# Retention and squared-ReLU FFN on one core: other idle matmuls, a merged first product, and work moved between the steps of the first block

## The chip, the cores and the metric

The kernel runs on one core of a Trainium2 chip. The metric is the device time of one execution in microseconds. A core has a matrix engine (PE, with its weight loads shown apart as PEld), a vector engine (DVE), a scalar engine (ACT), a general engine (POOL), a queue for transfers (SP), and 16 DMA engines which the queues of SP and POOL share. Each engine works through its own instructions in order and waits on semaphores for the others.

## The reference, cut to what matters

Four sequences of 768 tokens, 8 heads of 64. Each head keeps a decaying 64 x 64 state; its output goes through an FFN of width 2048 with a squared ReLU.

```python
gamma = 1.0 - 2.0 ** (-5.0 - np.arange(H))
for t in range(S):
    state = gamma[None, :, None, None] * state + np.einsum('bhd,bhe->bhde', k[:, :, t], v[:, :, t])
    y[:, :, t] = (1 / np.sqrt(D)) * np.einsum('bhd,bhde->bhe', q[:, :, t], state)
x = y.transpose(0, 2, 1, 3).reshape(B * S, H * D)        # 3072 x 512
h = np.maximum(x @ w_in, 0.0)                            # 3072 x 2048
out = (h * h) @ w_out                                    # 3072 x 512
```

## The kernel before

The 3072 tokens are 24 chunks of 128. Within a chunk the recurrence is turned into matmuls: q is scaled by powers of gamma and k by inverse powers, scores of k against q are masked to the causal half (DVE writes `pt`), the state of all earlier tokens stands in `c_ps` and is copied to `s_bd`, and the outputs are `s_bd` against q plus v against `pt`. The outputs, copied to `xt` by ACT or DVE, are the input of the FFN. Chunks are grouped into blocks for the FFN: the first has four chunks, the others two (`BLOCKS`).

There is no scheduler: the order in which the Python code issues instructions is the order on each engine (`manual_schedule`). Three parts matter here.

*The start, written out by hand from L1203.* Chunks 0 to 3 are handled as two pairs (0, 1) and (2, 3), in which a row of a tile holds two neighbouring tokens r=0 and r=1. `scale_q4`, `transpose_q4`, `scale_pair_k`, `transpose_pair_k`, `scores_pair`, `state_pair`, `outputs_pair` and `finish_pair` are the steps; `cast_pair_v(m, r)` turns the v of one r to bf16 on POOL, or on ACT with `on_scalar`. `outputs_pair` takes for each of two groups of heads first all matmuls of r=0 (eight), then those of r=1. Between the steps `keep_awake(n)` issues idle matmuls, 4n of 128 columns each, from a zeroed corner of the tile `spare` into a PSUM tile that nobody reads; `spare` is needed later for the masked scores of the second pair and for sums of the first block. `cast_w` turns quarters of w_in, which come by DMA as f32 into `stage`, to bf16, in halves of 256 columns, on the engines named by letters (V for DVE, S for ACT, G for POOL).

*The first product.* `first_product` multiplies one 128-column block f of w_in with `xt`, in four matmuls over the 512 inputs. `first_unit(tb, g, c, parts)` does the four blocks of quarter g for one chunk c, in two parts of two blocks, and then a ReLU by ACT (`relu`, L855) from PSUM into `h`; squares are taken by DVE (L826) at the next place. At the start, quarter 0 is done chunk by chunk: part 0 of chunks 0 and 1 ahead of the outputs of the second pair, part 1 after them, then chunks 2 and 3 whole. The other three quarters, f = 4 to 15, are done with 512 columns, all four chunks at once.

*The numbered places.* The FFN is a sequence of pieces, and after piece n the steps that `put` has noted for place n are issued. Places 5 to 16 follow the blocks f = 4 to 15 of the first block; 17 to 32 follow the pieces of its second product (`last_of_first`, `second_products`). There chunks 0 and 1 are done plainly, two rows f at a time (`plain`, L1039), and chunks 2 and 3 by a scheme of seven products on sums of h (`first_sums`, `third_sums`, `fourth_sums`) and of w_out (`sum_w_out`, L341), in 256-column matmuls (L1004). Its pieces are, by place: 17 to 20 plain(0) to plain(3), 21 the lower halves of two sum products, 22 and 23 plain(4) and plain(5), 24 a third lower half, 25 plain(6), 26 plain(7) followed by ACT's copy `a` of one product and two output copies, 27 two upper halves and DVE's u = product + a, 28 and 29 the product with `a12`, 30 and 31 a product that goes into the tile that u was read from, 32 the last. `third_sums` and `fourth_sums` are put at 26 and 27.

Among these pieces stand the steps of chunks 4 to 7: `attend(m, scaled, places)` puts `scale_kv` at the first place (DVE scales k, POOL casts v), `transpose_k` at the second (PE, then two ACT copies into `k_bd`, L426), the scores of two groups of heads at the third and fourth, `state` at the fourth, and `outputs` at the last (PE, then ACT's copy to `xt`, L529). From chunk 8 on another form is used (`attend2`), with half-chunk tables `kf2` and `cmask2` which `pack_constants` makes in two steps: memsets, iotas and masks on POOL, then a cast and a product on DVE and an exponential on ACT. On POOL's queue `load_w_out` issues the four quarters of w_out at places 6, 8, 11 and 14.

Of the kernel before, what the change touches and what calls it, by code (L numbers as in the profile page):

```python
# [9 lines left out]
FP32 = mybir.dt.float32  # L10
BF16 = mybir.dt.bfloat16
# [20 lines left out]
def kernel(  # L32
# [9 lines left out]
    nc = tc.nc  # L42
    P = nc.NUM_PARTITIONS
# [3 lines left out]
    C = 128  # L47
# [25 lines left out]
    hpool = ctx.enter_context(tc.tile_pool(name="hpool", bufs=3))  # L73
# [6 lines left out]
    ps_y = ctx.enter_context(tc.tile_pool(name="ps_y", bufs=1, space=bass.MemoryType.PSUM))  # L80
    ps_c = ctx.enter_context(tc.tile_pool(name="ps_c", bufs=1, space=bass.MemoryType.PSUM))
    ps_f = ctx.enter_context(tc.tile_pool(name="ps_f", bufs=4, space=bass.MemoryType.PSUM))
# [113 lines left out]
        load_w_in(g)  # L196


    spare = hpool.tile([P, 4096], BF16, name="h2")
    still = spare[:, 4096 - P : 4096]  # L200
    nc.vector.memset(still, 0.0)

    lng = const.tile([P, H], FP32)
    for h in range(H):
        nc.gpsimd.memset(lng[:, h : h + 1], float(np.log(gammas[h])))
# [34 lines left out]
    ident = const.tile([P, P], BF16)  # L240
# [115 lines left out]

    idle_ps = []

    def keep_awake(n, pool=ps_f, name="psf"):
        if not idle_ps:  # L360
            idle_ps.append(pool.tile([P, P], FP32, name=name))
        for _ in range(4 * n):
            nc.tensor.matmul(idle_ps[0][:], lhsT=still, rhs=still, start=True, stop=True)  # L363

    def end_awake():
        idle_ps.clear()
# [170 lines left out]
    def pair_view(t):  # L537
        return t.rearrange("s c hh d -> s (c hh d)").rearrange("s (r h d) -> s r h d", r=2, h=H)
# [42 lines left out]
    def cast_pair_v(m, r, on_scalar=False):  # L581
        at[m]["v"] = pair_view(v_bd2s[m // 2])
        if on_scalar:
            nc.scalar.activation(at[m]["v"][:, r], raw_v[m][:, r], AF.Copy)
        else:
            nc.gpsimd.tensor_copy(at[m]["v"][:, r], raw_v[m][:, r])
# [242 lines left out]
    h2s = {}  # L829

    def h_tiles(tb):
        wide = BLOCKS[tb] * C
        count = NFB * wide // 4096
        for _ in range(count):
            t = hpool.tile([P, 4096], BF16, name="h2")
            h2s.setdefault(tb, []).append(t.rearrange("e (f t) -> e f t", t=wide))

    def h_of(tb, f0, f1=None):
        n = NFB // len(h2s[tb])
        j, f = divmod(f0, n)  # L840
        return h2s[tb][j][:, f : f + (1 if f1 is None else f1 - f0)]

    def first_product(tb, hp, f, cols):
        g, fq = divmod(f, FPQ)
        for cb in range(NCB):
            nc.tensor.matmul(  # L846
                hp,
                lhsT=w_in_bf[g][:, cb, fq * 128 : (fq + 1) * 128],
                rhs=xts[tb][:, cb, cols],
                start=(cb == 0),  # L850
                stop=(cb == NCB - 1),
            )

    def relu(hv, hp, on_scalar=False):
        nc.scalar.activation(hv, hp[:], AF.Relu)  # L855
        squares.append((hv, on_scalar))
# [246 lines left out]
    def first_unit(tb, g, c, parts=(0, 1)):  # L1103

        if tb not in h2s:
            h_tiles(tb)
        if (tb, g, c) not in open_ps:
            open_ps[tb, g, c] = ps_f.tile([P, FPQ, C], FP32, name="psf")
        hp = open_ps[tb, g, c]
        cols = slice(c * C, (c + 1) * C)  # L1110
        half = FPQ // 2
        for part in parts:
            for fq in range(part * half, (part + 1) * half):
                first_product(tb, hp[:, fq, :], g * FPQ + fq, cols)
        if 1 in parts:
            relu(h_of(tb, g * FPQ, (g + 1) * FPQ)[:, :, cols], open_ps.pop((tb, g, c)))

    def ffn_pieces(tb):
        nch = BLOCKS[tb]
        TB = nch * C  # L1120
        if tb == 0:
            first_sums, last_sums, second_products = last_of_first()
            put(11, first_sums, 0)
            put(17, first_sums, 1)
            put(26, last_sums[0])
            put(27, last_sums[1])
            for f in range(FPQ, NFB):
                hp = ps_f.tile([P, TB], FP32, name="psf")
                first_product(tb, hp[:], f, slice(0, TB))
                relu(h_of(tb, f)[:, 0], hp)  # L1130
                yield
            yield from second_products()
            return
        elif tb <= 2:

            for c in range(nch):
                for g in range(NQ):
                    first_unit(tb, g, c)
                    if c * NQ + g in (1, 2, 3) and kept:
                        next(kept[0])  # L1140
                    if c * NQ + g == 4:
                        kept.clear()
                    if tb in SEVEN and (c, g) == (1, 3):
                        first_sums, rest = seven_products(tb)
                        first_sums(slice(0, 4))
                    yield
            if tb in SEVEN:
                yield from rest()
                return
        else:  # L1150
            h_tiles(tb)
            per = 512 // TB
            if tb in SEVEN:
                first_sums, rest = seven_products(tb)
            for f0 in range(0, NFB, per):
                hp = ps_f.tile([P, per, TB], FP32, name="psf")
                for f in range(f0, f0 + per):
                    first_product(tb, hp[:, f - f0, :], f, slice(0, TB))
                relu(h_of(tb, f0, f0 + per), hp, tb in SEVEN and f0 // per in (1, 3))
                if f0 // per in (1, 2, 3) and kept:  # L1160
                    next(kept[0])
                if f0 // per == 4:
                    kept.clear()
                if f0 // per == 5 and tb in SEVEN:
                    first_sums(slice(0, 4))
                yield
            if tb in SEVEN:
                yield from rest()
                return


        def second(op, j, g, cols=slice(0, DM)):
            for fq in range(FPQ):
                f = g * FPQ + fq
                nc.tensor.matmul(  # L1175
                    op[:],
                    lhsT=h_of(tb, f)[:, 0, j * C : (j + 1) * C],
                    rhs=w_out_bf[g][:, fq, cols],
                    start=(f == 0),
                    stop=(f == NFB - 1),  # L1180
                )

        def store(op, j, cols=slice(0, DM)):
            osb = opool.tile([P, DM], FP32, name="osb")
            nc.scalar.activation(osb[:, cols], op[:], AF.Copy)
            r0 = (first[tb] + j) * C
            nc.sync.dma_start(out[r0 : r0 + C, cols], osb[:, cols])


        for j in range(nch):  # L1190
            op = ps_f.tile([P, DM], FP32, name="psf")
            for g in range(NQ):
                second(op, j, g)
                if g == NQ - 1:
                    store(op, j)
                yield
# [3 lines left out]
    def small_pt():  # L1200
        return ptpool.tile([P, NPAIR, 2, C], BF16, name="pt").rearrange("s p hh t -> s (p hh t)")

    keep_awake(10, pool=ps_y, name="y")  # L1203
    scale_q4(0, 0)
    scale_q4(0, 1)
    transpose_q4(0, 0, *tp)
# [39 lines left out]
    state_pair(0, 1, "SV")  # L1246
    cast_w("in", 0, (0,), "GGGG")
    cast_pair_v(2, 0)
    cast_pair_v(2, 1, on_scalar=True)
    first_unit(0, 0, 0, (0,))  # L1250
    first_unit(0, 0, 1, (0,))
    cast_w("in", 0, (1,), "GGVV")
    outputs_pair(2, 0, ((ps_y, "y"), st))
    outputs_pair(2, 1)
    finish_pair(2, 0)
    state_pair(2, 0, "VV")
    first_unit(0, 0, 0, (1,))
    first_unit(0, 0, 1, (1,))
    finish_pair(2, 1, on_scalar=False)
    cast_w("in", 1, (0,), "VVGG")  # L1260
    first_unit(0, 0, 2)
# [9 lines left out]
    start = [sum(npieces[:tb]) for tb in range(len(BLOCKS) + 1)]  # L1271
    parts = {}

    def put(place, what, *args):
        parts.setdefault(place, []).append((what, args))
# [4 lines left out]
    def attend(m, scaled, places):  # L1280
        if m % 2 == 0:
            put(scaled, scale_q, m, 0)
            put(scaled + 2 if m == 4 else scaled, scale_q, m, 1)
            put(places[0], transpose_q, m)
        put(16 if m == 4 else places[0], scale_kv, m)
        put(places[1], transpose_k, m)
        put(places[2], scores, m, 0)
        put(places[3], scores, m, 1)
        put(places[3], state, m)
        put(places[4], outputs, m)  # L1290
# [23 lines left out]
    put(20, sum_w_out, 0)  # L1314
    put(22, sum_w_out, 1, (0, 1), slice(0, 2))
    put(24, sum_w_out, 1, (0, 1), slice(2, 4))
    put(26, sum_w_out, 1, (2, 3))
    attend(4, 12, (17, 19, 21, 23, 28))
    attend(5, None, (25, 28, 30, 32, 34))
    attend(6, 30, (33, 35, 37, 39, 42))  # L1320
    attend(7, None, (38, 42, 44, 46, 49))
    packed = pack_constants()
    put(27, next, packed)
    put(34, next, packed)
    for j, t in enumerate([s_bds[2]] + ks_bd2s + v_bd2s):
        for hh in range(2):
            put(35 + 2 * j + hh, zero_off_diagonal, t, hh)
# [35 lines left out]
    n = BLOCKS[0]  # L1363
# [36 lines left out]
```

## Time and profile before

| | |
|---|---|
| three runs | 204.14, 203.9, 203.99 us; median 203.99 |
| the profiled execution | 203.7 us, of it the span from first to last instruction 201.9 |
| granted clock of PE | 1.00 |
| idle matmuls, L363 | 72 of 128 columns; 217 to 314 ns each |
| first product, L846 | 879 recorded: 512 of 256 columns, 320 of 128, 47 of 512 |
| last landing of the second pair's v | 14.6 us |
| longest waits of PE | 1.0 us at the start for the zeroed tile, then 0.3 and 0.2 |

A row of the timeline gives the start in microseconds from the span's start, the time from the first start to the last end, the engine, the line, the operation with output and inputs and their shape, and how many were merged; in brackets stands idle time ahead of it and what ended it. Ends of matmuls are modelled and include the way through the array, so consecutive ones overlap; their pace is read from starts. A few matmul records are missing (47 recorded of 48 with 512 columns), which looks like a hole of one matmul.

### The profile page before, as it was taken

The numbers are of one execution on the slowest core, as the hardware profiler recorded it, in microseconds if no ns is written. First come the engines' busy times: TensorE is split into PE (matmuls) and PEld (weight loads), VectorE is DVE, ScalarE is ACT, GpSimd is POOL, SyncE is SP. The second block draws the span as 40 slices with busy tenths as digits, with TensorE's granted clock in tenths as the row PEclk, the third lists the DMA queues.
The fourth block names the chain that finished last, engine by engine and source line by source line (L and its number), as shares of the span: only waits on it lengthen the run. The fifth ranks groups of instructions, "written<-read, shape, count | busy, mean of one in ns | idle before, by whom it ended". The sixth has DMA issues, their size and how long they took to land.

```text
span 201.9 us, 5925 instructions
## 1 busy us (share of the span) xinstructions
PE 196.4 (97%) x2403; PEld 167.2 (83%) x2408; DVE 148.5 (74%) x315; ACT 127.8 (63%) x259; POOL 81.1 (40%) x152
## 2 busy tenths in 40 slices
PE   8999999999999999999999999999999999999993
PEld 8688445669965998999999999999899999999883
DVE  3987899789684678777787777777787687485374
ACT  8775875164852766783785785783775766863730
POOL 8675721099930973362622084224382022200000
PEclk9999999999999999999999999999999999999999
DMA  5999999999799999889999789999999572200202
GB/s 171 356 371 398 337 200 196 252 246 291 201 229 234 103 137 160 153 202 201 211 183 221 134 145 167 230 178 204 178 148 167 157 107 54 109 0 3 104 3 106
DMA packets 92252, 36.57 MB, mean 181 GB/s; under 512 B 68544, under 2 KB 88256, under 8 KB 92224
## 3 DMA queue, kind: packets, MB, share of 16 engines
q1 hardware_dynamic: 77312, 32.52, 68.7%
q0 software_dynamic: 14912, 3.67, 20.6%
q8 instruction: 19, 0.31, 0.6%
q14 instruction: 9, 0.07, 0.1%
HBM read 27.26 MB, written 6.29 MB: 166 GB/s over the span
## 4 chain that ended last, share of the span: by engine, by line
PE 94%; DVE 2%; ACT 1%; issue 1%; DVEq 0%
PE psf L846 42%; PE psf L880 18%; PE tp L880 7%; PE psf L1175 3%; PE psf L1039 3%; PE y L363 3%; PE psf L1004 3%; PE st L747 2%; PE y L803 2%; PE y L796 2%; PE c_ps L774 2%; PE c_ps L642 1%; PE st L445 1%; PE y L521 1%; DVE osb L876 1%
## 5 line engine op out<-in xcount | busy, mean ns | idle before, releaser
L846 PE MATMUL psf<-xt,w_in_bf 128*128 128x256 bf16 (+2 forms) x879 | 92.3, 259 | 0.1
L846 PEld LDWEIGHTS <-w_in_bf 128*128 128x128 bf16 x880 | 71.2, 98 | 11.2
L855 ACT ACTIVATE h<-psf 128x512 bf16<-128x512 f32 x96 | 56.2, 595 | 21.2 <-PE psf L846 18.9
L725 POOL COPY v_bd<-v 64x512 bf16<-64x512 bf16 x32 | 21.5, 673 | 73.7 <-DVE v L717 64.8
L826 DVE TENSOR_TENSOR h<-h 128x512 bf16<-128x512 bf16 x80 | 33.6, 433 | 21.1 <-ACT h L855 20.5
L880 PEld LDWEIGHTS <-h 128*128 128x128 bf16 x288 | 26.5, 98 | 3.0 <-DVE h L826 0.3
L160 POOL DMA_DIRECT2D k_big<-in_k_dram x32 | 21.0, 674 | 0.0
L880 PE MATMUL psf<-w_sum,h 128*128 128x256 bf16 x136 | 19.1, 273 | 0.0
L880 PE MATMUL tp<-w_out_bf,h 128*128 128x256 bf16 x136 | 19.1, 273 | 0.0
L880 PE MATMUL psf<-w_sum,k_bd 128*128 128x256 bf16 x144 | 17.9, 273 | 0.0
L876 DVE TENSOR_TENSOR u<-psf,u 128x256 f32<-128x256 f32 x18 | 7.6, 424 | 11.3 <-PE psf L880 10.9
L880 PEld LDWEIGHTS <-k_bd 128*128 128x128 bf16 x144 | 13.8, 98 | 1.5
L783 ACT ACTIVATE s_bd<-c_ps 64x256 bf16<-64x256 f32 x29 | 10.7, 370 | 6.5 <-PE c_ps L774 6.5
L876 DVE TENSOR_TENSOR osb<-psf,u 128x256 f32<-128x256 f32 x26 | 10.3, 422 | 6.1 <-PE psf L880 5.8
L376 DVE TENSOR_TENSOR qs<-qn,qf 128x512 bf16<-128x512 f32 x20 | 14.0, 704 | 0.4 <-DMA qn<-in_q_dram 0.4
L784 ACT ACTIVATE s_bd<-c_ps 64x256 bf16<-64x256 f32 x29 | 11.0, 379 | 0.4
L754 DVE TENSOR_TENSOR pt<-st,cmask 128x512 bf16<-128x512 f32 x16 | 11.0, 688 | 0.1
L717 DVE TENSOR_TENSOR v<-stage,kf 128x512 bf16<-128x512 f32 x16 | 11.0, 684 | 0.0
L916 ACT ACTIVATE osb<-tp 128x256 f32<-128x256 f32 x8 | 3.1, 385 | 12.2 <-PE tp L880 12.2
L810 ACT ACTIVATE xt<-y 128x512 bf16<-128x512 f32 x16 | 9.6, 598 | 1.8 <-PE y L803 1.2
L824 ACT ACTIVATE h<-h 128x512 bf16<-128x512 bf16 x16 | 10.1, 630 | 0.5
L876 DVE TENSOR_TENSOR k_bd<-h 128x512 bf16<-128x512 bf16 x18 | 10.1, 559 | 0.3
(151 smaller groups left out, 304.7 us busy)
## 6 DMA issues: line engine op xcount, KB each, us to landing
qn<-in_q_dram SPq DMA_DIRECT2D x12, 512.0 KB, 5.5
out_dram<-osb SPq DMA_DIRECT2D x23, 256.0 KB, 2.8
stage<-in_v_dram SPq DMA_DIRECT2D x32, 96.0 KB, 4.5
stage<-in_moe_w_in_dram SPq DMA_DIRECT2D x4, 512.0 KB, 7.6
stage<-in_moe_w_in_dram SPq DMA_DIRECT2D x2, 1024.0 KB, 8.1
w_out_bf<-in_moe_w_out_dram POOLq DMA_DIRECT2D x4, 512.0 KB, 10.2
kn<-in_k_dram SPq DMA_DIRECT2D x6, 256.0 KB, 6.0
k_big<-in_k_dram POOLq DMA_DIRECT2D x32, 48.0 KB, 4.3
```

The lines of the kernel that those rows point to most:

```text
L160: nc.gpsimd.dma_start(t[rows, :, p, hh, :], k[b, 2 * p + hh, (i + 3 * n) * C : (i + 3 * n + 3) * C].rearrange("(w s) d -> s w d", s=64),)
L376: engine.tensor_tensor(out=out, in0=by, in1=table[:, :, None].to_broadcast([P, H, D]), op=ALU.mult)
L717: nc.vector.tensor_tensor(out=v2.rearrange("s (u p) d -> s u p d", u=2), in0=vn, in1=kf2[:, i, :, :, None].to_broadcast([P, 2, NPAIR, D]), ...
L725: nc.gpsimd.tensor_copy(v_bd[rows, :, hh, :], v2[rows])
L754: nc.vector.tensor_tensor(out=pt[:], in0=st[:], in1=cmask2.rearrange("s r t -> s (r t)")[:, None, :].to_broadcast([P, 2 * NPAIR, C // 2]), ...
L783: nc.scalar.activation(s_bd[halves[0], :, 0, :], c[halves[0]], AF.Copy)
L784: nc.scalar.activation(s_bd[halves[1], :, 1, :], c[halves[1]], AF.Copy)
L826: nc.vector.tensor_mul(hv, hv, hv)
L846: nc.tensor.matmul(hp, lhsT=w_in_bf[g][:, cb, fq * 128 : (fq + 1) * 128], rhs=xts[tb][:, cb, cols], start=(cb == 0), stop=(cb == NCB - 1),)
L855: nc.scalar.activation(hv, hp[:], AF.Relu)
L876: nc.vector.tensor_tensor(out=out, in0=in0, in1=in1, op=op)
L880: nc.tensor.matmul(to, lhsT=left[:, j], rhs=right(j) if callable(right) else right[:, j], start=(start and j == 0), stop=(stop and j == NF ...
```

## The change

Five edits.

1. `keep_awake` now issues n matmuls of 512 columns instead of 4n of 128. Weights and moving data are the identity tile `ident`, read four times over. The zeroed corner and its memset are gone, `spare` is made just ahead of the start, and the first call has n = 7 instead of 10.
2. `first_pair(part)` does two blocks f for chunks 0 and 1 together, 256 columns a matmul, with a ReLU of its own, in place of `first_unit` on each of the two chunks.
3. `cast_pair_v(2, 1)` runs on POOL, behind `cast_pair_v(2, 0)`, instead of on ACT.
4. The outputs of chunk 4 move from place 28 to 24, the transposes of chunk 5's k from 28 to 27, and the last difference of w_out (`sum_w_out` with 3) from 26 to 27, behind `third_sums` and u on DVE.
5. The two steps of `pack_constants` move from places 27 and 34 to 12 and 15. On POOL the first then stands between the third and the fourth `load_w_out`.

```diff
-    spare = hpool.tile([P, 4096], BF16, name="h2")
-    still = spare[:, 4096 - P : 4096]
-    nc.vector.memset(still, 0.0)
...
-    def keep_awake(n, pool=ps_f, name="psf"):
+    def keep_awake(n, width=4 * C, pool=ps_f, name="psf"):
         if not idle_ps:
-            idle_ps.append(pool.tile([P, P], FP32, name=name))
-        for _ in range(4 * n):
-            nc.tensor.matmul(idle_ps[0][:], lhsT=still, rhs=still, start=True, stop=True)
+            idle_ps.append(pool.tile([P, 4, P], FP32, name=name))
+        wide = max(1, width // C)
+        for _ in range(n):
+            nc.tensor.matmul(
+                idle_ps[0][:, 0:wide, 0 : width // wide],
+                lhsT=ident[:],
+                rhs=ident[:, None, 0 : width // wide].to_broadcast([P, wide, width // wide]),
+                start=True,
+                stop=True,
+            )
...
+    def first_pair(part):
+
+        if 0 not in h2s:
+            h_tiles(0)
+        hp = ps_f.tile([P, 2, 2 * C], FP32, name="psf")
+        for n in range(2):
+            first_product(0, hp[:, n, :], 2 * part + n, slice(0, 2 * C))
+        relu(h_of(0, 2 * part, 2 * part + 2)[:, :, 0 : 2 * C], hp)
...
-    keep_awake(10, pool=ps_y, name="y")
+    spare = hpool.tile([P, 4096], BF16, name="h2")
+    keep_awake(7, pool=ps_y, name="y")
...
     cast_pair_v(2, 0)
-    cast_pair_v(2, 1, on_scalar=True)
-    first_unit(0, 0, 0, (0,))
-    first_unit(0, 0, 1, (0,))
+    cast_pair_v(2, 1)
+    first_pair(0)
...
-    first_unit(0, 0, 0, (1,))
-    first_unit(0, 0, 1, (1,))
+    first_pair(1)
...
-    put(26, sum_w_out, 1, (2, 3))
-    attend(4, 12, (17, 19, 21, 23, 28))
-    attend(5, None, (25, 28, 30, 32, 34))
+    put(26, sum_w_out, 1, (2,))
+    put(27, sum_w_out, 1, (3,))
+    attend(4, 12, (17, 19, 21, 23, 24))
+    attend(5, None, (25, 27, 30, 32, 34))
...
-    put(27, next, packed)
-    put(34, next, packed)
+    put(12, next, packed)
+    put(15, next, packed)
```

## The prediction

> **What bounds the kernel now.** I read the page's first part, its chain of waits, the waits of PE, and then the instructions in order of time, above all where the chain leaves PE.
>
> ```profile
> span 201.9 us, 5925 instructions
> PE 196.4 (97%) x2403; PEld 167.2 (83%) x2408; DVE 148.5 (74%) x315; ACT 127.8 (63%) x259; POOL 81.1 (40%) x152
> PE 94%; DVE 2%; ACT 1%; issue 1%; DVEq 0%
> ```
>
> PE sets the end: the chain runs on PE for 94% of the span. An edit pays only if it takes columns from PE or closes a hole in PE's row. Holes are few; these two lines of PE's waits are the ones that the change aims at:
>
> ```profile
> PE st L445 <- ACT k_bd L426: 0.3, 1, 0.3
> PE psf L1004 <- DVE u L1000: 0.2, 1, 0.2
> ```
>
> A busy PE here includes about 0.17 us of drain behind the last matmul of a group, so the true holes are longer. In order of time (start, length, engine, line):
>
> ```profile
> 43.53 0.60 PE L1004 MATMUL psf<-w_out_bf,h 128*128 128x256 bf16 x4
> 43.86 0.42 DVE L1000 TENSOR_TENSOR u<-psf,u 128x256 f32<-128x256 f32 x1
> 44.00 1.20 ACT L426 ACTIVATE k_bd<-tp 64x512 bf16<-64x512 bf16 x2
> 44.34 0.60 PE L1004 MATMUL psf<-w_sum,h 128*128 128x256 bf16 x4 [0.21 <-DVE u L1000]
> 44.77 0.22 PE L445 MATMUL st<-qT,k_bd 128*128 128x128 bf16 x1
> 45.25 0.34 PE L445 MATMUL st<-qT,k_bd 128*128 128x128 bf16 x3 [0.26 <-ACT k_bd L426]
> ```
>
> Four 256-column matmuls take 0.44 (L1004's eight before outputs(5) run from 48.83 to 49.70, 0.87), so PE stands from 43.97 to 44.34 for u, 0.37, and from 44.83 to 45.25 for the second k_bd copy, 0.42. Together 0.79 us, and only this is to be won here. The start looks like this:
>
> ```profile
> 14.26 0.90 PEld L846 LDWEIGHTS <-w_in_bf 128*128 128x128 bf16 x16
> 14.64 0.61 POOL L586 CAST v_bd<-vn 128x512 bf16<-128x512 f32 x1 [1.31 <-DMA vn<-in_v_dram]
> 14.77 0.63 ACT L584 ACTIVATE v_bd<-vn 128x512 bf16<-128x512 f32 x1
> 15.30 0.51 PEld L666 LDWEIGHTS <-v_bd 64*64 64x64 bf16 x32
> 15.91 0.23 PEld L682 LDWEIGHTS <-s_bd 128*128 128x128 bf16 x4
> ```
>
> The v of chunks 2 and 3 lands at 14.6; POOL turns row half r=0 to bf16 until 15.25 and ACT r=1 until 15.40; PE takes r=0 at 15.30 and its ninth matmul, the first of r=1, at 15.45. From 14.26 on PE is in its row without a free stretch over 0.2 us until 43.97, so a delay here is carried on.
>
> **Wide idle matmuls.** The memset of L201 goes (0.11 on DVE, which then waits for POOL's iota anyway: 0). The idle work now reads ident, ready at 1.84 + 0.29 = 2.13, and starts about 2.2 instead of 1.00. At the start 40 matmuls of 128 columns take 4.18 of weight loads, 0.105 each; 7 of 512 columns are 28 such, 2.9 us, and end near 5.1. The first transposes wait for qs until 5.45 in any case. Between them one of 512 columns (0.216, from L1039's four and one in 0.97) stands for four of 128 (0.056 each, 0.90 for 16): nothing. So 0, if the clock keeps its moment: the four transposes at 5.45 take 0.61, the next four at 6.05 take 0.40, so full speed came near 5.9. The bounds are in the rivals.
>
> The profile's granted clock is 1.00 in every stretch and doesn't show the slow time; the rows do. [...]
>
> **Chunks 0 and 1 merged, r=1 to POOL.** 32 matmuls of 128 columns become 16 of 256: 1.79 becomes 16 x 0.109 = 1.75, gain 0.04 (eight of 256 take 0.87), which the wait below takes back. The first pair needs both xt; the second is written by ACT at 13.85 + 0.59 = 14.44, so it starts at 14.49, not 14.26, and ends at 15.36; r=0 follows at about 15.46. Then r=1: POOL's two casts of the same shape at 10.56 take 1.16 together, so r=1 is ready at 14.64 + 1.16 = 15.80 and seen at 15.85, where PE sees 15.45 now: **+0.40**. Behind it stand L682, state, the second pair, and by DVE (s_bd at 16.90, xt at 18.25) first_unit(0,0,3); each follows its predecessor within 0.1, so all move. POOL's next cast waits for DMA until 15.93: no cost. ACT is free 0.63 earlier, but its next work waits for PE: no gain. Bounds: 0, if a later wait swallows it, to +0.45.
>
> **Tables sooner.** POOL's 2.3 us (40.95 to 43.22) now stands between w_out's third and fourth issue, at 25.7. The fourth lands 39.2 at the latest of four that land one after another, each 3.4 apart; issued 2.3 later it is still queued before its turn. Its first users are L1039 at 39.38, which moves back by 0.67, and L341 at 40.10. DVE's two (0.17 + 0.50) and ACT's 0.24 move into the stretch at 30 to 32, where DVE has no free time until 36.09, but then 0.67 before the mask at 36.76. The tightest user is the second sum, done 34.48, used by PE at 35.46 + 0.44 = 35.90: 1.4 to spare. A POOL operation beside DVE can cost as much again (L341 took 1.10 beside a POOL cast, 0.69 else). Cost 0; were DVE 1.4 later, PE would wait for the rest, so up to +0.2. The later k_big memsets end 2.3 earlier: nothing waits.
>
> **Outputs of chunk 4, u and k of chunk 5.** In the times of before; the +0.40 shifts them all. outputs(4), 0.67 (42.64 to 43.31), is put in at 39.38. Its third head pair needs the mask done at 39.61, and comes at 39.72: no wait, but only 0.06 to spare. The two plain pieces run 40.05 to 42.00, the upper sums 0.87 to 42.87, k's transposes 0.22 to 43.09, L1004's eight 0.88 to 43.97, then the four that need u. DVE: w_sum ends 42.48, two sums 0.79 to 43.25, u 0.42 to 43.67, w_sum's last and the fourth sums after it. u is there 0.3 before 43.97: the 0.37 hole goes. Then scores(5,0) at 44.41. ACT: a at 42.00 + 0.20 = 42.20, the two osb copies at 42.48 and 42.96, k_bd at 43.45 and 44.05, the second ready at 44.65, seen at 44.70 (xt, now 0.60 of ACT's time before them, is done long before). PE's second score matmul thus starts at 44.70 instead of 45.25: **-0.55**, and of the 0.79 a hole of 0.24 stays, behind the osb copies. The mask behind it starts 45.08 (DVE's fourth sums end 45.0), as far behind the scores as now. Bounds: -0.79 if ACT is quicker, 0 if outputs(4) waits for its mask or the k_bd copies slip.
>
> **Sum.** 0 + 0.40 + 0 - 0.55 = -0.15. The profiled run took 203.7 (span 201.9 and 1.8 around it); so 203.55 for such a run, a span of 201.75; the median of the runs shown is 203.99, 0.29 above it, so I forecast **203.84**, one part in a thousand. No change can be told under 0.2%, which is 0.41 us.
>
> **Rivals.**
> 1. *The wait for r=1 is hidden.* The second pair today starts at 16.79 and waits for a w_in cast, ending 16.86, whose data came by DMA at 15.9; a chain hung on DMA alone would take up the delay. Then only the middle counts: 203.99 - 0.55 = 203.44. Against it: L666, L682, L642 and L846 follow one another with no more than 0.1 between them, so PE and not DMA leads. 0.28.
> 2. *The middle doesn't pay.* outputs(4) waits for its mask, or ACT's copies come late, and the hole only moves: 203.99 + 0.40 = 204.39. For it: 0.06 to spare at the mask; ACT's four copies in a row. Against: ACT and DVE were idle (2.0 before u, 0.69 before the mask). 0.12.
> 3. *Slower: the clock comes late.* Idle work starts 1.2 later and is a third shorter. If that isn't enough to lift the clock, PE runs slow through the thin stretch from 5.95 to 14.26. There it has 82 whole matmuls and 96 quarter ones, about (82 + 24) x 0.056 = 5.9 of work in 8.31; at 0.105 each only half of 8.31, 4.2, gets done; 1.7 is left over, less the 0.3 that PE would stand for r=1 anyway: 205.4 and more. It decides from a clock later than about 7.5, when the lag (0.2 per us) passes that cover. For it: the start moves by 1.2. Against: from 2.2 to 5.1 PE is as dense as before, and a slow PE stays dense. 0.10.
>
> That the change doesn't do what it says is seen for one part only: the merge saves 0.04 of PE.
>
> **How the numbers follow.** The forecast holds 0.50, of which 0.07 falls below -0.41 and 0.03 above +0.41; rival 1 has 0.28 (0.05 of it within), rival 2 0.12, half within, rival 3 0.10. Faster 0.07 + 0.23 = 0.30; slower 0.03 + 0.06 + 0.10 = 0.19; the rest, 0.51, can't be told from no change. The range goes from both gains whole (-0.79 and no cost at the start, near 203.1 to 203.2) to rival 2 with DVE's 0.2 and a little of rival 3, 204.8.
>
> **What would show it.** L666's weight loads split, with a wait for POOL before r=1 until about 15.85; the 512-column first product starting at about 20.9, not 20.53; no wait for u; a wait of 0.2 to 0.3 for k_bd; transposes at 6.05 at 0.10 or less each. Wrong would be: the first products of chunk 2 no later than 18.04, a hole over 0.4 before the scores of chunk 5, or slow transposes after 7.

## The result, and the profile after

The changed kernel took 203.18 us in the median of 12 executions (203.13 to 204.40); before took 204.01 in as many (203.89 to 204.48). The ratio is 0.9969, with a 95% interval from 0.9958 to 0.998: faster by 0.3%, where -0.15 us had been forecast and -0.83 came. The 12 do not lie around one value: nine are at 203.13 to 203.32, called early below, and three at 204.07 to 204.40, called late. The profiled one is a late one, at 204.40: its profile has a start that most executions don't have, and a hole of 0.28 at 48.5 which the early executions profiled below lack.

The page of the changed kernel, its first lines and the chain of waits by engine:

```profile
span 202.6 us, 5780 instructions
PE 195.3 (96%) x2330; PEld 162.8 (80%) x2335; DVE 147.8 (73%) x314; ACT 127.5 (63%) x258; POOL 81.3 (40%) x153
PE 90%; DVE 4%; DMA 2%; ACT 2%; issue 1%; DVEq 0%
```

PE's longest waits in it (line, releaser, us in total, times, longest):

```profile
PE y L360 <- POOL ident L238: 2.2, 1, 2.2
PE c_ps L602 <- DVE ks_bdp L577: 1.0, 1, 1.0
```

PE still sets the end. The idle matmuls now wait 2.2 us for the identity tile (1.0 for the zeroed corner before). The waits for u and for chunk 5's k copies are gone from the list, and a wait of 1.0 for a scaled k at the start is new.

The middle, in order of time (start, length, engine, line):

```profile
44.15 1.04 PE L1007 MATMUL psf<-w_out_bf,h 128*128 128x256 bf16 x8
44.20 0.42 DVE L1003 TENSOR_TENSOR u<-psf,u 128x256 f32<-128x256 f32 x1
44.48 1.21 ACT L429 ACTIVATE k_bd<-tp 64x512 bf16<-64x512 bf16 x2
45.02 0.60 PE L1007 MATMUL psf<-w_sum,h 128*128 128x256 bf16 x4
45.45 0.63 PE L448 MATMUL st<-qT,k_bd 128*128 128x128 bf16 x4
45.74 0.17 PEld L448 LDWEIGHTS <-k_bd 128*128 128x128 bf16 x3 [0.29 <-ACT k_bd L429]
```

u is ready at 44.62, 0.4 before the four matmuls that need it, and these follow the eight without a hole (44.15 + 0.87 = 45.02). The second k copy ends at 45.69; PE stands from 45.51 to 45.74, 0.23, where a hole of 0.24 was foretold.

The start:

```profile
13.47 1.18 POOL L589 CAST v_bd<-vn 128x512 bf16<-128x512 f32 x2
...
15.43 1.03 PE L849 MATMUL psf<-xt,w_in_bf 128*128 128x256 bf16 x8 [0.16 <-ACT xt L697]
```

POOL's two casts of the second pair's v start at 13.47 and end at 14.65. In before POOL stood 1.31 us for that v and began at 14.64. So r=1 was there before PE wanted it, and the +0.40 of the forecast did not come.

### The profile page after: what moved, and what is told of

Its sections match the earlier page's. It is cut to its first block, busy times and chain, and to the rows that moved or that the text cites. A ratio compares the mean times of both kernels' runs of the same rounds, so it can differ in the third digit from the quotient of the medians.

```text
span 202.6 us, 5780 instructions
## 1 busy us (share of the span) xinstructions
PE 195.3 (96%) x2330; PEld 162.8 (80%) x2335; DVE 147.8 (73%) x314; ACT 127.5 (63%) x258; POOL 81.3 (40%) x153
## 4 chain that ended last, share of the span: by engine, by line
PE 90%; DVE 4%; DMA 2%; ACT 2%; issue 1%; DVEq 0%
PE psf L849 41%; PE psf L883 18%; PE tp L883 7%; PE psf L1187 3%; PE psf L1042 3%; DMA qn<-in_q_dram 2%; PE y L806 2%; PE st L750 2%; PE y L799 2%; PE c_ps L777 2%; PE psf L1007 2%; PE y L360 1%; PE y L524 1%; PE st L448 1%; PE c_ps L645 1%; DVE qs L379 1%
## 5 line engine op out<-in xcount | busy, mean ns | idle before, releaser
L829 DVE TENSOR_TENSOR h<-h 128x512 bf16<-128x512 bf16 x80 | 33.1, 427 | 22.3 <-ACT h L858 21.8
L379 DVE TENSOR_TENSOR qs<-qn,qf 128x512 bf16<-128x512 f32 x20 | 14.8, 745 | 0.0
```

The source lines that it names most:

```text
L379: engine.tensor_tensor(out=out, in0=by, in1=table[:, :, None].to_broadcast([P, H, D]), op=ALU.mult)
L829: nc.vector.tensor_mul(hv, hv, hv)
```

## The experiments

**The changed kernel again (e1_after)**, unchanged:

> The changed kernel itself, for the trace of an execution that took about 203.15 us (of twelve executions nine took 203.13 to 203.32 and three 204.07 to 204.40; the trace at hand is of one with 204.40, in which the transposes stay slow until about 7.8 us). Fetch theory: the second pair's v lands near 13.4 as in the trace at hand, not at 14.6 as before, since a fetch of 16 KB of instructions no longer falls into that transfer (it stood at 11.9 before and at 15.7 now); so POOL has both casts done by about 14.7, PE doesn't wait for r=1, and the first 512-column product starts about 20.2 to 20.4 where the clock comes early, against 20.53 before. Rival, the prediction's own step: r=1 waits until about 15.85 and that product starts at 20.9; then the middle must have given about 1.2 us instead of 0.55.

Median 203.18 of 11: six at 203.09 to 203.18, five at 204.02 or more (one of 205.66). With the 12 above, 8 of 23 executions lie about 1 us over the others. The profiled one, 204.44, is again one of the late ones and shows the same start as the first. v landed at 13.39, as the fetch theory has it. The start of 20.2 to 20.4 that it expects in early executions did not come in those profiled below (20.62 and 20.68): v's earlier landing by itself brings the start nothing.

**Narrow idle matmuls in the changed kernel (e2_narrow)**

```diff
+    spare = hpool.tile([P, 4096], BF16, name="h2")
+    still = spare[:, 4096 - P : 4096]
+    nc.vector.memset(still, 0.0)
...
-        for _ in range(n):
-            nc.tensor.matmul(
...
+        for _ in range(4 * n):
+            nc.tensor.matmul(idle_ps[0][:], lhsT=still, rhs=still, start=True, stop=True)
...
-    keep_awake(7, pool=ps_y, name="y")
+    keep_awake(10, pool=ps_y, name="y")
```

> The changed kernel with the idle matmuls of before (zeroed corner, 4n of 128 columns, first call n = 10), all other edits kept. Fetch theory: PE has 108 more instructions early, the fetch falls near 11.9 again, v lands near 14.6, r=1 waits for POOL until about 15.85, and the time is about 203.7 to 203.9, the value of my sum. Rival (the merge and POOL's cast cost nothing by themselves, the landing of v differs by chance): time as with the change, about 203.15. Clock theory, which concerns the executions near 204.2 alone: idle work starts at 1.0 again, so all executions lie within 0.3 us of each other.

Median 204.49, spread from 203.54 to 205.60, so both theories missed: the time is not 203.7 to 203.9, and the executions are not within 0.3 of each other, although idle work starts at 1.00. What spreads them is open. The trace (203.76, full speed at 6.43) is clear on one thing: v's last part landed at 14.60 again, as in before. What r=1 on POOL costs then it doesn't show, for in this execution the second q landed at 7.15, where the 13 other profiles have 6.66 to 6.77. PE came to r=1 0.6 later than in before, at 16.05, and POOL was done at 15.82.

**Only the wide idle matmuls, on before (e3_wide_only)**: edit 1 of the diff and nothing else.

> The kernel before with the wide idle matmuls alone. Fetch theory: v lands near 13.4, first products of chunk 0 start about 14.3 as before, the outputs of the second pair no longer wait, and the w_in cast behind them comes 1.1 earlier too: 0.2 to 0.3 less than before, about 203.75, with some executions near 1 us longer, in which the clock comes late. Rival (idle matmuls do nothing to the time, the gain is that of the middle): 204.0.

Theory and rival both fell: median 204.49, ratio 1.0026 (1.0017 to 1.0035), so this edit alone loses. v landed at 13.35, and the first 512-column product started at 20.57, no later than in before (20.53). The loss lies behind that, in holes against those of e5_before (below): 0.36, where there was none, ahead of plain(6), whose quarter of w_out landed at 39.75 and was wanted at 39.43; 0.56 instead of 0.42 at chunk 5's scores; 0.27 instead of 0.16 at chunk 6's; less 0.23 at u, where 0.15 is left of 0.38.

**r=1 cast on ACT, as before (e4_act_cast)**

```diff
-    cast_pair_v(2, 1)
+    cast_pair_v(2, 1, on_scalar=True)
```

> The changed kernel with r=1 of the second pair's v on ACT again. Fetch theory: POOL's two casts end at about 14.65 with the change, before PE comes, so nothing changes: 203.15 within 0.1. Rival (PE does wait for POOL's second cast, as predicted): 0.3 to 0.4 faster, about 202.8.

Seven of 12 at 203.14 to 203.43, five at 204.10 to 204.81. Its best, 203.14, and the changed kernel's, 203.09, are the same within what can be told: which engine casts r=1 is worth nothing here. The profiled execution was an early one (203.19, span 201.4): its 512-column products start at 20.68.

**Before again (e5_before)**, unchanged, with a new profile:

> The kernel before, unchanged, profiled a second time beside the others. The profiled execution of the prediction had a span of 201.93 us, while most timed executions on the last chip showed 202.0 to 202.3. Theory (the start of before waits for v, whose second transfer is held up by a 16 KB instruction fetch on one DMA engine): the fetch stands near 11.9 us, v's second transfer lands near 14.6, the first 512-column product starts at 20.5 to 20.8, median 203.9 to 204.0. Rival (the profiled execution was an odd one): v lands near 13.4 and the fetch lies elsewhere.

Median 204.02, span 202.3. v landed at 14.79. The execution that the prediction was made from had a span of 201.93, shorter than all 12 of these (202.1 to 202.7). Its 512-column products start 0.17 earlier (20.53 against 20.70), and it lacks a hole of 0.16 at chunk 6, of which more below.

**Wide idle matmuls that start early (e6_early_wide)**

```diff
+    spare = hpool.tile([P, 4096], BF16, name="h2")
+    still = spare[:, 4096 - P : 4096]
+    nc.vector.memset(still, 0.0)
...
-                lhsT=ident[:],
-                rhs=ident[:, None, 0 : width // wide].to_broadcast([P, wide, width // wide]),
+                lhsT=still,
+                rhs=still[:, None, 0 : width // wide].to_broadcast([P, wide, width // wide]),
...
-    keep_awake(7, pool=ps_y, name="y")
+    keep_awake(10, pool=ps_y, name="y")
```

> The changed kernel with wide idle matmuls that read a zeroed corner of the spare tile, so that they start near 1.0 us as in before, and with ten of them in the first call. The arithmetic of the outputs is unchanged. Theory A (what separates the executions of the changed kernel near 203.15 from those near 204.2 is the moment at which TensorE's clock comes to full speed; idle matmuls from 1.0 us on bring it before 6.5 every time): at least 9 in 10 executions between 203.0 and 203.5, median 203.2, span of a profiled one near 201.4. Theory B (few instructions at the start, not the early clock, is what moves the instruction fetch): the fetch is behind 14 us and v's second transfer lands near 13.4; if instead the fetch follows the moment at which TensorE starts, it lies near 11.9, v lands near 14.6 and the time is 203.5 to 203.8. Rival (the two levels have another cause): the same mix as the changed kernel, about a third of the executions at 204.0 or more.

All five executions at 203.14 to 203.21, span 201.4 in each: none is late. PE's idle work begins at 1.00 instead of 2.19, and it is longer too, ten matmuls instead of seven; the run doesn't part the two. v landed at 13.37. Five executions are few: at 8 late ones in 23, five early ones in a row come by chance about once in eight times. In e10_late_tables and e11_no_merge (below), which start in the same way, 2 of 12 each lie 0.6 to 1.0 above their median. So late executions seem rarer, 4 of these 29; that they are gone is not shown.

**No first idle matmuls (e7_no_first_idle)**

```diff
-    keep_awake(7, pool=ps_y, name="y")
...
-    keep_awake(1)
+    keep_awake(1, pool=ps_y, name="y")
```

> The changed kernel without its first call of idle matmuls, so that TensorE has nothing to do before 5.5 us or so. The arithmetic of the outputs is unchanged. Theory A (a late clock costs the changed kernel about 1 us): full speed at 8 us or later in every execution, the mask of the first pair at 8.8 or later, the first 512-column product at 21.5 or later, median 204.2 to 205.5 and hardly an execution under 203.6. Rival (the clock's moment is hidden and the two levels have another cause): the same mix as the changed kernel, median near 203.2.

Median 204.53 of 12, from 204.11 to 208.10, and the 512-column products start at 22.08: theory A held. PE's transposes show the clock; in the timeline of e7_no_first_idle four of them take 0.61 to 0.63 up to the one at 11.00, and 0.39 from the next:

```profile
5.47 0.61 PE L568 MATMUL tp<-ident,qs 128*128 128x128 bf16 x4 [5.47 <-DVE qs L551]
...
11.00 0.63 PE L602 MATMUL c_ps<-ident,ks_bdp 128*128 128x128 bf16 x4
12.14 0.39 PE L602 MATMUL psf<-ident,ks_bdp 128*128 128x128 bf16 x4
```

The trace's clock records put full speed at 11.61. So I take the moment of full speed for what splits the executions of the changed kernel: in its two profiles, both of late executions, it came at 7.79 and 8.11, in the early execution of e4_act_cast at 4.97, with the same first idle matmul at 2.19. Why the moment differs between such executions is not shown. It was 4.19 to 6.52 in the nine profiles whose idle work starts at 1.00, 4.97 to 8.11 in the four that start at 2.19, and 11.61 for a start at 5.47. The full-speed stretches of the 14 traces last 191.15, 194.56 or 197.97 us, two steps of 3.41.

How a late clock costs 1 us is seen by laying the same lines of the changed kernel and of e6_early_wide side by side. The changed kernel, full speed at 7.79:

```profile
8.84 0.69 DVE L626 TENSOR_TENSOR pt<-st,maskp 128x512 bf16<-128x512 f32 x1 [0.80 <-PE psf L618]
9.45 1.23 DVE L577 TENSOR_TENSOR ks_bdp<-kn,kfp 128x512 bf16<-128x512 f32 x1
10.73 0.40 PE L602 MATMUL c_ps<-ident,ks_bdp 128*128 128x128 bf16 x4 [1.01 <-DVE ks_bdp L577]
```

e6_early_wide, full speed at 4.19 (its lines are numbered 4 higher):

```profile
8.36 0.69 DVE L630 TENSOR_TENSOR pt<-st,maskp 128x512 bf16<-128x512 f32 x1 [0.31 <-PE psf L622]
9.01 0.69 DVE L581 TENSOR_TENSOR ks_bdp<-kn,kfp 128x512 bf16<-128x512 f32 x1
9.76 0.40 PE L606 MATMUL c_ps<-ident,ks_bdp 128*128 128x128 bf16 x4
```

The matmuls ahead of full speed (four transposes take 0.61 at 6.09, against 0.40 at 6.03 in e6_early_wide) make DVE's first mask 0.48 late. DVE's scaling of k, next on its queue, then starts at 9.45 instead of 9.01, and takes 1.23 instead of 0.69. Together PE gets the scaled k 0.97 later, and the 512-column products start at 21.58 instead of 20.62. On POOL the second of two scalings of another k runs beside it. In the changed kernel that one starts at 9.09, 0.36 ahead of DVE's, and takes 1.04 to DVE's 1.23. In before it starts at 9.07, 0.05 behind DVE's at 9.02, and takes 1.55 to DVE's 0.69; in e2_narrow, at 9.54 against 9.49, the same 1.55 and 0.69. In e6_early_wide POOL's two scalings take 2.95 together, where they take 2.44 in the changed kernel. That the scaling which starts first holds the other one up is my reading; the rows show the starts and the lengths alone. e4_act_cast, whose code is the changed kernel's but for the later cast of r=1, shows the same with its early clock: mask at 8.33, scaling of k 0.69 from 9.09.

The profiled late executions lose 0.28 more in the middle. The changed kernel at chunk 6's q:

```profile
46.73 1.70 DVE L379 TENSOR_TENSOR qs<-qn,qf 128x512 bf16<-128x512 f32 x2
47.17 0.72 POOL L395 CAST v_bd<-vn 128x512 bf16<-128x512 f32 x1
47.98 0.90 PE L409 MATMUL tp<-ident,qs 128*128 128x128 bf16 x8
```

Shifted by 1 us, DVE's scaling of q runs beside POOL's cast of v and takes 1.70, where e6_early_wide has 1.28 and PE's eight transposes take 0.61. 0.96 at the start and 0.28 here are the whole difference of the spans, 202.63 against 201.38. e7_no_first_idle, later still, has no such hole.

**Only the moves in the middle, on before (e8_middle_only)**: edit 4 without edit 5.

```diff
-    put(26, sum_w_out, 1, (2, 3))
-    attend(4, 12, (17, 19, 21, 23, 28))
-    attend(5, None, (25, 28, 30, 32, 34))
+    put(26, sum_w_out, 1, (2,))
+    put(27, sum_w_out, 1, (3,))
+    attend(4, 12, (17, 19, 21, 23, 24))
+    attend(5, None, (25, 27, 30, 32, 34))
```

> Before, with only chunk 4's outputs at place 24, chunk 5's k at place 27 and the sum of w_out's second half split over places 26 and 27. Theory (the middle alone gives 0.55 to 0.65, the start is that of before): median 203.3 to 203.5, second score matmul at 44.7 if the 512-column products start at 20.53, a hole of about 0.24 left ahead of chunk 4's first outputs. Rival (the gain comes from the start alone, the middle is paid back at a later wait): median 203.9 to 204.0.

The theory fell: median 203.92, no change to be told from the 204.05 of before beside it. The rival was right that the middle is paid back at a later wait, and wrong that the start brings a gain (20.57 here). The second score matmul is at 44.74, 0.68 sooner than in e5_before, so the hole did go; the gain is lost again eight microseconds later. The timeline of e8_middle_only at chunk 6:

```profile
50.33 0.17 DVE L214 CAST ex_k_f<-ex_k_i 128x48 f32<-128x48 int32 x1
50.54 1.06 DVE L215 TENSOR_TENSOR ex_k_f<-ex_k_f,lng 128x48 f32<-128x48 f32 x1
50.94 0.60 POOL L392 CAST v_bd<-vn 128x512 bf16<-128x512 f32 x1
51.64 0.24 ACT L300 ACTIVATE kf<-ex_k_f 128x48 f32<-128x48 f32 x1 [0.98 <-DVE ex_k_f L215]
52.26 1.20 ACT L426 ACTIVATE k_bd<-tp 64x512 bf16<-64x512 bf16 x2
53.51 0.34 PE L445 MATMUL st<-qT,k_bd 128*128 128x128 bf16 x3 [0.39 <-ACT k_bd L426]
```

The half form's table (ex_k_f, kf) is made here at place 34, and its small operations stand ahead of chunk 6's k copies in ACT's queue. DVE's product, 0.21 where it is alone (e9_middle_tables, at 31.20), takes 1.06 and ends 0.06 behind POOL's cast of v; ACT waits 0.98 for it; the copies end at 53.46, and PE stands 0.13 + 0.56 = 0.69.

**Both moves, without wide idle matmuls and merge (e9_middle_tables)**: before with edit 4, shown above, and edit 5:

```diff
-    put(27, next, packed)
-    put(34, next, packed)
+    put(12, next, packed)
+    put(15, next, packed)
```

> Before, with the moves in the middle (chunk 4's outputs at 24, chunk 5's k at 27, the sum of w_out split) and the half form's tables at 12 and 15; idle matmuls and first products as in before. Theory (the two moves need each other: the tables' small operations stand ahead of chunk 6's k copies in ACT's queue, and with the tables late the middle's gain is lost at the first score matmuls of chunk 6): first 512-column product at 20.5 to 20.7, second score matmul of chunk 5 at 44.7 to 44.9 with a hole of 0.23, no hole at chunk 6's score matmuls near 52.9, a hole of about 0.1 instead of 0.2 near 58.4, span 201.3 to 201.5, median 203.1 to 203.3. The wide idle matmuls and the merge then bring nothing. Rival (they carry part of the gain): median 203.5 to 203.9.

Five executions at 203.09 to 203.20, median 203.15. The theory held in each point: first 512-column product at 20.64, second score matmul at 44.81, no hole at chunk 6, the hole at 58.3 down to 0.09 from 0.20. Chunk 6's k copies now end at 52.7, before PE comes:

```profile
51.52 1.20 ACT L426 ACTIVATE k_bd<-tp 64x512 bf16<-64x512 bf16 x2
52.83 0.39 PE L445 MATMUL st<-qT,k_bd 128*128 128x128 bf16 x4
```

These two edits are the whole gain; the other three add nothing to them (203.18 with all five). Edit 5 alone was not run.

**The tables back (e10_late_tables)**: e6_early_wide with edit 5 undone.

> The changed kernel with the early wide idle matmuls of the second call, and the half form's tables back at places 27 and 34. Theory: PE waits 0.5 to 0.7 us at chunk 6's score matmuls near 52.9 for k_bd, behind the table's operation on ACT, and the hole near 58.4 is back at 0.2; span 202.0 to 202.2, median 203.8 to 204.0. Rival (the tables cost nothing where they are, as the prediction had it): median 203.2, no hole at 52.9.

Median 203.96, ten of 12 at 203.92 or more; the profile shows the same 1.06 of DVE's product, and holes of 0.69 at chunk 6 and 0.20 at 59.1. Two executions came out at 203.06 and 203.07. That in these two DVE's product came through beside POOL is my reading; neither was profiled.

**First products apart again (e11_no_merge)**: e6_early_wide with the four `first_unit` calls in place of `first_pair`.

> The changed kernel with the early wide idle matmuls, and the first products of chunks 0 and 1 apart again, 128 columns each; the second pair's v is cast on POOL as in the changed kernel. Theory (the merged products wait 0.2 us for the second chunk's xt, and v is there in time): the first product starts at 14.27 instead of 14.47, the first 512-column product at 20.45 to 20.5 instead of 20.62, median 203.0 to 203.05. Rival (something else sets the start, or PE waits for r=1): 20.6, median 203.17.

The theory fell again: the first product started at 14.22 and the second pair's s_bd matmuls at 15.79 instead of 16.00, as expected, but the median is 203.47, and the 512-column products start at 20.95. The lost time is in one place, inside a run of state matmuls that wait for nothing on any engine:

```profile
16.12 0.45 PE L649 MATMUL c_ps<-v_bd,ks_bdp 64*128 64x128 bf16 x5
16.96 0.32 PE L649 MATMUL c_ps<-v_bd,ks_bdp 64*128 64x128 bf16 x3 [0.38 <-issue]
```

In starts the hole is 0.57. e3_wide_only has three idle matmuls and their weight loads fewer, and there a wait on "issue" ends at 16.97, six instructions further on, at the start of the next product: in both kernels PE stands after its 449th recorded instruction. An instruction fetch of 16 KB starts at 14.65 and 14.70 in them. e6_early_wide, whose merged products are eight matmuls and eight weight loads fewer by then, comes to its 449th at 17.33 and has no such hole; e12_scores_later, with the start of e11_no_merge, has it at 16.96 again. I read it as PE out of instructions until the fetched ones could be used, 2.3 us after the fetch began; the profile itself names no cause.

**Chunk 5's first scores one place later (e12_scores_later)**: e11_no_merge with

```diff
-    attend(5, None, (25, 27, 30, 32, 34))
+    attend(5, None, (25, 27, 31, 32, 34))
```

> The kernel of the run before in this call, with chunk 5's first score matmuls one place later (31 for 30), so that four products with w_sum of the next piece lie between chunk 5's k copies on ACT and the score matmuls that wait for them. Theory (the hole of 0.23 us left behind the osb copies is a wait for k_bd alone): no hole there, median 202.75 to 202.85. Rival (chunk 5's mask on DVE comes later, behind qs of chunk 6, and PE waits for it or for the score tile at the second score matmuls): a new hole of 0.1 to 0.3 at 45.9, median 202.95 to 203.15.

Median 205.21, worse by 1.74 than e11_no_merge. The hole of 0.23 is gone, and one of 2.03 took its place:

```profile
45.25 1.29 DVE L383 TENSOR_TENSOR qs<-qn,qf 128x512 bf16<-128x512 f32 x2
45.26 0.39 PE L452 MATMUL st<-qT,k_bd 128*128 128x128 bf16 x4
...
47.25 0.68 DVE L459 TENSOR_TENSOR pt<-st,cmask 128x512 bf16<-128x512 f32 x1
47.98 0.38 PE L452 MATMUL st<-qT,k_bd 128*128 128x128 bf16 x4 [1.87 <-DVE pt L459]
```

The mask of the first scores fell behind chunk 6's q, a u and an osb on DVE's queue, and the second scores wait for that mask. The rival was right in kind, and its 0.1 to 0.3 far too small.

## Why the prediction was right in the middle and wrong in the sum

- **"Outputs of chunk 4, u and k of chunk 5": -0.55.** Right. From e5_before to e9_middle_tables the second score matmul goes from 45.42 to 44.81; 0.06 of that is the start (20.70 against 20.64), 0.55 the middle. The hole left is 0.23, foretold 0.24. What the step missed is that it stopped there. What would be late next stood in the rows of before:

```profile
50.89 0.50 DVE L215 TENSOR_TENSOR ex_k_f<-ex_k_f,lng 128x48 f32<-128x48 f32 x1
52.06 1.19 ACT L426 ACTIVATE k_bd<-tp 64x512 bf16<-64x512 bf16 x2
53.27 0.39 PE L445 MATMUL st<-qT,k_bd 128*128 128x128 bf16 x4
```

Chunk 6's second k copy ends at 53.25, and PE, which begins these scores at 53.27, loads it at 53.30: next to nothing to spare. A PE that comes 0.55 sooner finds it late.
- **"Tables sooner": cost 0.** It cost nothing, but it was worth something, and this is one of the two steps that failed in the sum. Between e10_late_tables and e6_early_wide it is 203.96 - 203.17 = 0.79, from holes of 0.69 and 0.11 that close; without it edit 4 is worth 204.05 - 203.92 = 0.13. Even with edit 4 undone the late table costs PE 0.16 in e5_before, where the small cast ahead of the product takes 0.64 beside POOL's cast. In the execution that I predicted from the hole was absent, so nothing in PE's waits pointed at it; the product's 0.50 did, for an operation of this line and shape takes 0.21 at 1.56. w_out's fourth quarter landed at 39.38 in the changed kernel (39.19 in before), ahead of its first use behind the moved outputs, as the step had it.
- **"Chunks 0 and 1 merged, r=1 to POOL": +0.40.** Wrong, measured 0 (first 512-column product at 20.62 in e6_early_wide, 20.64 in e9_middle_tables). The working rested on v landing at 14.6. This is the other step that failed. In before 15 of v's 16 parts land by 13.39 and one at 14.58; a packet of instructions of 16,384 bytes starts at 11.92 and takes 0.95, and I take it to hold that part up. With 57 idle matmuls and their 57 weight loads fewer at the start the fetch comes later, at 15.65 in the changed kernel, and v is whole at 13.42. The second step of the same paragraph, that the merged pair waits for the second xt and starts at 14.49, was right (14.47). What r=1 on POOL costs when v lands at 14.6 stays open (e2_narrow). And the merge is not idle: next to wide idle matmuls it saves 20.95 - 20.62 = 0.33, by the hole of 0.57 on "issue" that e11_no_merge has and e6_early_wide doesn't.
- **"Wide idle matmuls": 0.** Right for 15 of 23 executions. In the two of the other 8 that were profiled rival 3 is seen to happen, from the point it named (full speed at 7.79 and 8.11; it decided from about 7.5), and I take the six for the same; but it costs 0.8 to 1.3 us (one execution of 205.66 apart), not the 1.4 and more that 205.4 stood for. Its price was a lag of 0.2 per us of slow matmuls alone (0.105 each against 0.056). With full speed at 7.79 that lag is about half of it, 0.48 at the first mask; the rest is DVE's scaling of k there, begun behind POOL's (1.23 for 0.69) and, in the profiled ones, 0.28 more at chunk 6's q. In e7_no_first_idle, with full speed at 11.61, DVE's scaling takes 0.68 again, and the lag alone puts the 512-column products 1.46 behind those of e6_early_wide; 7.4 us later at 0.2 are 1.5, so the lag was priced rightly, and the longer scaling was what rival 3 lacked. The median shows 204.53 - 203.17 = 1.36.
- **The sum.** Forecast 0 + 0.40 + 0 - 0.55 = -0.15. Measured, from the trace of e5_before to that of e9_middle_tables: 0.06 at the start, 0.55, 0.16 at chunk 6 and 0.11 at 59, together 0.88, against spans of 202.3 and 201.4. Rival 1, 203.44, was the nearest of the cases; it lacked the 0.27 of the tables. 203.18 lies at the low end of the range, which began at 203.1. That it lies inside is in part luck: the low end stood for 0.79 from the holes at u and at chunk 5's k, and what came was 0.55 from these and 0.27 from the tables, for which the sum had no term. A change that can't be told had been given 0.51, and faster, which came, 0.30.

No version beat the changed kernel's own early executions. But 203.15 and 203.17, with no execution at 204 among five each, are had from e9_middle_tables and e6_early_wide, the first with two of the five edits.

## What to carry to other kernels

After a stall is closed on the engine that sets the end, look for the next operand that arrives with almost nothing to spare: here a copy 8 us further on, and the small table operations queued ahead of it decided whether the gain stayed. One move was worth 0.13 alone and 0.83 together with the other, so a part that brings nothing when tried by itself is not yet refuted. Look at when idle matmuls begin and how long they last: seven from 2.19 on left 8 of 23 executions about 1 us longer, ten from 1.00 on none of five.

## What the runs showed of the hardware

*A packet of instructions among the data, and a late part of v.* The list of DMA queues of before for the stretch from 11 to 14.6 us has one packet of instructions among 1824 of data (queue, kind: packets, MB, share); that of the changed kernel has none there:

```profile
q1 hardware_dynamic: 1824, 1.30, 109.9%
q8 instruction: 1, 0.02, 1.7%
```

The packet has 16,384 bytes and takes 0.95 us; in the changed kernel one of the same size starts at 15.65 and takes 0.96. Where it falls into the transfer of v, in the five profiles with narrow idle matmuls, the last of v's 16 parts lands between 14.58 and 14.79, and the others by 13.43 (in e2_narrow one more is late, 13.85); where it comes at 14.65 or later, all have landed by 13.42. The fetch went with the number of instructions that PE had begun: over the 14 profiles it starts anywhere from 11.85 to 16.36, but always when 293 to 353 instructions of PE have begun (309 in before, 336 in the changed kernel). With fewer of them issued a transfer's end came 1.2 us sooner (14.58 in before, 13.42 in the changed kernel). That the packet holds the late part up is my reading; which DMA engine carried the two is not shown. If the reading of e11_no_merge is right, PE stood for such a fetch too, 0.57.

*A DVE operation of 0.21 us can take 1.06 beside POOL.* In e8_middle_only it ends with POOL's cast of v, which reads `vn`; in e5_before the same product takes 0.21 beside POOL's memsets, which only write. What makes it longer is not shown. The product is recorded from 50.54, 0.40 before the cast's own start. In e5_before DVE's small cast ahead of the product, which has one input, takes 0.64 beside POOL's cast, where e8_middle_only has 0.17. Both the runs leave unexplained.
